# A fixed order of all tasks and loads in a fused retention and feed-forward kernel

## The chip, the cores and the metric

One core of a Trainium2 chip. The metric is the device time of one launch in microseconds (us): the median of three runs of the kernel before is 216.17 us, the runs lie between 215.56 and 217.98. The profiled run took 216.75 us and its span, from the first to the last instruction of the program, is 215.0 us.

## The reference

```
state = gamma * state + k[:, :, t] (outer) v[:, :, t]        # 4 batches, 8 heads, 768 steps, head size 64
y[:, :, t] = scale * q[:, :, t] @ state
x  = y as [4, 768, 512]                                       # heads side by side
xn = (x - mean(x)) / sqrt(var(x) + 1e-6) * g_ln
out = x + max(xn @ w_ch1, 0) @ w_ch2                          # w_ch1 512 x 2048, w_ch2 2048 x 512
```

Inputs and output are float32; the kernel works in bfloat16 with float32 sums.

## The kernel before, in words

**Tiles.** The 4 x 768 rows are cut into 24 tiles of 128 rows, t = 0 to 23: tiles 0 to 3 are the first chunk of each batch, tiles 4 to 8 are chunks 1 to 5 of batch 0, tiles 9 to 13 those of batch 1, and so on. The recurrence is worked in chunks: within a tile as a masked product, between tiles through a state.

**Tasks of one tile.** For t below 8 the tile's k and q are transposed on TensorE (PE) into PSUM (`tk` L440, `tq` L447) and copied out by ScalarE (`ek`) and VectorE (`eq` L452). From tile 8 on, k and q are loaded side by side into a buffer `qk` and transposed by a DMA issued by SyncE (`tr` L462). Then PE forms the scores (`pa` L480), VectorE masks them (`am` L491), PE forms the output y (`py`, L508 and, with a state, L504), VectorE takes mean and variance (`bn` L523, L524) and the shifted, scaled tile (`xn` L518), ScalarE keeps a copy of y (`xc` L529). The tile xn is transposed into a buffer `xnt`, on PE for t below 8 (`tx` L582, copy `ex` on ScalarE), by a SyncE DMA after that (`ex` L596). The state takes a product on GpSimd (`vg` L542), one on PE (`pd` L554) and one on VectorE (`pb` L568).

**The feed-forward.** Tiles are taken in 14 groups: eight of one tile, four of two, two of four. `m1(g, ho)` (L629) multiplies a group's xnt by a part of w1; each such task streams about 0.87 to 0.89 us of matmuls into one of two PSUM buffers `mm`. A `relu` task empties it into `h1` (ScalarE L642; for the first six groups ScalarE or VectorE L644). `m2(t)` (L667) multiplies h1 of one tile by w2 in four parts of four matmuls, into one of two PSUM buffers `tp`; VectorE adds the residual (`add` L676) and SyncE stores the tile (`st` L683). w1 and w2 come in four chunks each, W1_0 to W1_3 and W2_0 to W2_3; `m1(g, ho)` needs chunk W1_(ho/4), and the first part of any m2 needs all four chunks of w2.

**Loads.** GpSimd (POOL) issues all loads of k, q, v (L375, 128 KB each in bfloat16) and of w1 and w2 (L383, 512 KB each) into one queue. From tile 8 on, each load has a `gate` before it (L388): a tiny copy on POOL that waits until the load three earlier has landed. Only k and q of tile 0 come by the other queues, in two halves each, from SyncE and ScalarE (L346).

**Order.** The program has 818 tasks. Each is created by `a(...)` with the engine or engines that may run it, an estimated duration, a rank and its dependencies. `Plan.order` then places them one at a time: of all tasks that can start, it takes the one with the earliest estimated start, and among equals the lowest rank. The estimates add fixed margins for what a load or a DMA transpose may take (`load_pad`, `w_pad`, `tr_pad`, `x_pad`) and, for some tasks, a slack or a time before which they may not start (`slack`, `at`). The result is the order in which the instructions of each engine are written; on the chip an engine runs its own list in order and waits by semaphores. `Plan.fill` puts matmuls on zeros (`warm`, L694) into 80% of those gaps of PE that the plan shows in its first 14 us.

Of the kernel before, what the change touches and what calls it, by code (L numbers as in the profile page):

```python
# [14 lines left out]
PE, ACT, DVE, POOL, SP = range(5)  # L15
# [4 lines left out]
              "k3", "q3", "v3", "w1_2", "k4", "q4", "v4", "k5", "q5", "v5", "w1_3", "w2_0",  # L20
              "k6", "q6", "v6", "k7", "q7", "v7", "w2_1", "w2_2", "w2_3"],
    "bufs": {"qsb": 6, "ksb": 5, "vsb": 9, "qk": 8, "tr": 6, "vg": 3, "trq": 3, "trk": 3},
    "load_pad": 600, "w_pad": 1500, "lead": 32, "lead2": 32, "sq_at": 28000, "late_load": 1250, "tail": (0, 384, 512), "step": 8, "pace": 8, "ahead": 3,
    "slack": 600, "tr_pad": 4000, "x_pad": 3000, "vg_pad": 1000, "fill": 0.8, "fill_end": 14000,
}


class Plan:
# [20 lines left out]
        self.tasks.append(t)  # L49
        return t  # L50

    def order(self):
        left, ends = {}, {}
        for t in self.tasks:
            for u in t["uses"]:
                left[u] = left.get(u, 0) + 1
        held = {name: [] for name in self.bufs}
        engines = sorted(self.seen)
        free = dict(self.begin)
        todo = {e: [t for t in self.tasks if e in t["on"]] for e in engines}  # L60
        sw_free, hw_free, out = self.first_load, 0, []
        while any(todo.values()):
            best = None
            for e in engines:
                for t in todo[e]:
                    if any("end" not in d for d in t["after"] + t["follows"]):
                        continue
                    at = max(free[e], t["at"], sw_free - 7000 if t["load"] else 0)
                    for d in t["after"]:
                        if d["eng"] == e and not d["load"] and not d["hw"]:  # L70
                            at = max(at, d["end"])
                        else:
                            at = max(at, d["seen"] + t["slack"])
                    if t["takes"]:
                        name = t["takes"][0]
                        if len(held[name]) == self.bufs[name]:
                            oldest = held[name][0]
                            if left[oldest]:
                                continue
                            at = max(at, ends[oldest])  # L80
                    if best is None or (at, t["rank"]) < best[0]:
                        best = (at, t["rank"]), t, e
            if best is None:
                raise RuntimeError("no task can start")
            (at, _), t, e = best
            for x in t["on"]:
                todo[x].remove(t)
            t["eng"], t["start"], t["ns"] = e, at, t["on"][e]
            t["end"] = free[e] = at + t["ns"]
            t["seen"] = t["end"] + self.seen[e] + t["lat"]  # L90
            if t["load"]:
                sw_free = max(t["end"] + 800, sw_free) + t["load"]
                t["seen"] = sw_free + 700 + t["lat"]
            if t["hw"]:
                begun = max(at + 600, hw_free)
                queued = max(0, sw_free - begun)
                hw_free = begun + t["hw"] + min(queued, 2 * t["hw"])
                if queued:
                    sw_free += t["hw"] * 2 // 3
                t["end"] = free[e] = max(t["end"], hw_free - 900)  # L100
                t["seen"] = hw_free + 1050 + t["lat"]
            if t["takes"]:
                name = t["takes"][0]
                if len(held[name]) == self.bufs[name]:
                    held[name].pop(0)
                held[name].append(t["takes"])
            for u in t["uses"]:
                left[u] -= 1
                ends[u] = max(ends.get(u, 0), t["seen"])
            out.append(t)  # L110
        return out
# [16 lines left out]
def kernel(  # L128
# [28 lines left out]
    number = {bc: t for t, bc in enumerate(TILES)}  # L157
# [6 lines left out]
    FILL, FILL_END = CFG["fill"], CFG["fill_end"]  # L164
# [11 lines left out]
    plan = Plan({PE: 330, ACT: 130, DVE: 130, POOL: 130, SP: 0},  # L176
                {PE: 900, ACT: 800, DVE: 900, POOL: 840, SP: 740}, 3900)
# [18 lines left out]
    held = {}  # L196
# [93 lines left out]
    a = plan.add  # L290
# [105 lines left out]
    seq = [(x, t) for t in range(8) for x in "kqv"] + [("w1", j) for j in range(4)]  # L396
# [31 lines left out]
    for t in range(NT):  # L428
# [5 lines left out]
        slack = SLACK if t >= T0 else 0  # L434
# [25 lines left out]
        else:  # L460
            def e_tr(eng, t=t):
# [4 lines left out]
                   hw=1600, lat=TR_PAD)  # L466

            def e_eq(eng, t=t):
# [3 lines left out]
                   follows=[ams[-1]])  # L472
# [25 lines left out]
        def e_py(eng, t=t, c=c):  # L498
# [8 lines left out]
            for h in range(H):  # L507
# [7 lines left out]
                slack=slack)  # L515
# [76 lines left out]
        else:  # L592
            def e_ex(eng, t=t, xb=xb, xi=xi):
                if xi == 0:
# [4 lines left out]
                      follows=[ex[t - 1]] if xi else [])  # L599
# [95 lines left out]
                                 rhs=zeros[:, 0:w], start=True, stop=True)  # L695

    with tc.manual_schedule():
        for t in plan.fill(plan.order(), PE, 1100, FILL_END, FILL, warm):
            t["emit"](t["eng"])


# [28 lines left out]
```

## Time and profile before

| what | value |
|---|---|
| time, median of 3 | 216.17 us |
| span of the profiled run | 215.0 us |
| PE busy with matmuls | 206.0 us, 96% of the span, 1944 records |
| of it matmuls on zeros (L694) | 25 records, 7.3 us busy |
| VectorE, ScalarE, POOL busy | 118.2, 83.7, 97.7 us |
| POOL's load queue | 13.37 MB, 86.7% of 16 DMA engines' span |
| last load landed | about 141 us |

The profile counts a PE instruction as busy from its start to a modelled end, and neighbours overlap. The times at which successive matmuls start say more: the difference of two starts is what the first one really took from the end time. The second thing to look at is the idle time in brackets in the timeline, with what ended it.

### The profile page before, as it was taken

What the parts mean: (1) busy time and instruction counts of PE and PEld (TensorE: products, weight loads), DVE (VectorE), ACT (ScalarE), POOL (GpSimd) and SP (SyncE); (2) the same over time, 40 slices, a digit from 0 to 9 for tenths busy, and PEclk for the clock granted to TensorE, in tenths of its full rate; (3) what the DMA queues carried; (4) which work ended last, traced back from release to release, by engine and by line L of the source; (5) the groups of instructions that cost most, each with busy time, mean ns of one, the idle gap of its engine ahead of it and who ended that gap; (6) DMA issues with size and microseconds to landing.
All of it is one profiled execution on the core that took longest, in us unless ns stands there. A gap on an engine that the chain in (4) does not pass through costs nothing.

```text
span 215.0 us, 4757 instructions
## 1 busy us (share of the span) xinstructions
PE 206.0 (96%) x1944; PEld 132.5 (62%) x1964; DVE 118.2 (55%) x230; ACT 83.7 (39%) x157; POOL 97.7 (45%) x151
## 2 busy tenths in 40 slices
PE   7978999999999999999999999989999999999994
PEld 3457999998745558668567767645454544444443
DVE  6776688991178955186896857784164411011121
ACT  5366676665401106325325424305434214442000
POOL 8997779734767765686846485600000000000000
PEclk9999999999999999999999999999999999999999
DMA  8999999999899999999999999971112120010212
GB/s 125 174 180 180 164 195 169 208 118 138 90 155 179 179 173 203 145 166 136 149 139 179 139 172 164 148 181 26 24 49 73 27 98 19 30 47 5 98 49 98
DMA packets 108887, 26.82 MB, mean 125 GB/s; under 512 B 101569, under 2 KB 105921, under 8 KB 108866
## 3 DMA queue, kind: packets, MB, share of 16 engines
q0 software_dynamic: 77024, 13.37, 86.7%
q1 hardware_dynamic: 30642, 12.82, 27.8%
q10 hardware_dynamic: 1200, 0.33, 0.6%
q8 instruction: 15, 0.25, 0.4%
q14 instruction: 6, 0.05, 0.1%
HBM read 27.30 MB, written 6.29 MB: 156 GB/s over the span
## 4 chain that ended last, share of the span: by engine, by line
PE 82%; DMA 10%; POOL 5%; issue 1%; DVE 0%; POOLq 0%
PE tp L667 38%; PE mm L629 34%; DMA v<-in_v_dram 5%; DMA w<-in_moe_w_ch_dram 4%; PE pa L480 3%; PE pd L554 2%; PE py L508 2%; PE py L504 2%; POOL qsb L375 1%; DMA xnt<-xn 1%; POOL w L383 1%; POOL v L375 1%; POOL k L375 1%; POOL vg L542 0%; PE tp L582 0%
## 5 line engine op out<-in xcount | busy, mean ns | idle before, releaser
L629 PE MATMUL mm<-xnt,w 128*128 128x128 bf16 (+2 forms) x896 | 93.9, 257 | 1.4 <-ACT xnt L203 0.7
L667 PE MATMUL tp<-w,h 128*128 128x512 bf16 (+2 forms) x381 | 87.2, 370 | 1.3 <-issue 0.5
L642 ACT ACTIVATE h<-mm 128x512 bf16<-128x512 f32 x91 | 54.5, 598 | 72.9 <-PE mm L629 72.6
L629 PEld LDWEIGHTS <-w 128*128 128x128 bf16 x896 | 66.2, 98 | 21.5 <-issue 1.5
L667 PEld LDWEIGHTS <-h 128*128 128x128 bf16 x400 | 37.0, 98 | 38.3
L676 DVE SCALAR_TENSOR_TENSOR osb<-tp,rstd,x_all 128x512 f32<-128x512 f32 (+2 forms) x25 | 18.2, 729 | 48.1 <-PE tp L667 47.9
L491 DVE TENSOR_TENSOR asb<-pa,mask 128x1024 bf16<-128x1024 f32 x24 | 29.3, 1221 | 16.1 <-PE pa L480 16.1
L523 DVE BATCH_NORM_STATS2 bns<-py 128x6 f32<-128x512 f32 x24 | 16.7, 694 | 18.8 <-PE py L508 18.8
L529 ACT CAST x_all<-py 128x512 bf16<-128x512 f32 x24 | 14.0, 583 | 18.3 <-DVE xn L518 17.7
L542 POOL TENSOR_TENSOR vg<-vsb,vsc 128x512 bf16<-128x512 bf16 x16 | 16.6, 1044 | 6.0 <-DMA vsb<-in_v_dram 3.2
L375 POOL DMA_DIRECT2D vsb<-in_v_dram x20 | 18.3, 916 | 1.4 <-issue 1.4
L518 DVE SCALAR_TENSOR_TENSOR xn<-py,mv,gb 128x512 bf16<-128x512 f32 x24 | 18.0, 750 | 0.9
L568 DVE TENSOR_TENSOR state<-pd,gch 64x256 bf16<-64x256 f32 x40 | 16.7, 418 | 2.7 <-PE pd L554 2.4
L375 POOL DMA_DIRECT2D qk<-in_q_dram x16 | 14.0, 877 | 3.5 <-issue 2.8
L375 POOL DMA_DIRECT2D qk<-in_k_dram x16 | 14.1, 879 | 2.0 <-issue 1.7
L388 POOL COPY scrap<-qk 1x1 bf16<-1x1 bf16 x30 | 5.8, 194 | 16.3 <-DMA qk<-in_k_dram 8.6
L469 DVE TENSOR_TENSOR trq<-tr,qsc 128x512 bf16<-128x512 bf16 x16 | 7.9, 495 | 3.6 <-DMA tr<-qk 3.5
L604 ACT ACTIVATE rstd<-mv,epsb 128x1 f32<-128x1 f32 (+2 forms) x14 | 3.8, 289 | 13.7 <-DVE mv L524 13.7
L694 PE MATMUL pd<-zeros 128*128 128x512 bf16 (+1 forms) x25 | 7.3, 434 | 1.2 <-DVE zeros L238 1.2
L508 PEld LDWEIGHTS <-asb 128*128 128x128 bf16 x192 | 7.9, 98 | 0.5 <-issue 0.4
L508 PE MATMUL py<-vsb,asb 128*128 128x64 bf16 x160 | 7.9, 193 | 0.0
L504 PE MATMUL py<-state,trq 128*128 128x128 bf16 x80 | 7.7, 219 | 0.0
(64 smaller groups left out, 120.9 us busy)
## 6 DMA issues: line engine op xcount, KB each, us to landing
out_dram<-osb SPq DMA_DIRECT2D x23, 256.0 KB, 2.1
w<-in_moe_w_ch_dram POOLq DMA_DIRECT2D x8, 512.0 KB, 9.4
vsb<-in_v_dram POOLq DMA_DIRECT2D x20, 128.0 KB, 5.5
qk<-in_k_dram POOLq DMA_DIRECT2D x16, 128.0 KB, 4.8
qk<-in_q_dram POOLq DMA_DIRECT2D x16, 128.0 KB, 5.4
qsb<-in_q_dram POOLq DMA_DIRECT2D x7, 128.0 KB, 8.9
v<-in_v_dram POOLq DMA_DIRECT2D x4, 128.0 KB, 7.1
ksb<-in_k_dram POOLq DMA_DIRECT2D x4, 128.0 KB, 9.3
```

What stands on the lines that cost most here:

```text
L375: nc.gpsimd.dma_start(out=tile_of(kind, j), in_=src)
L491: nc.vector.tensor_tensor(out=take("asb", t, [P, NPAIR, 2, P], BF16).rearrange("p i a t -> p a i t"), in0=held["pa", t], in1=mask.rearrang ...
L508: nc.tensor.matmul(py[:, h, :], lhsT=held["asb", t][:, h // 2, h % 2, :], rhs=tile_of("v", t)[:, h, :], start=(mi == 0), stop=(mi == n - 1))
L518: nc.vector.scalar_tensor_tensor(out=take("xn", t, [P, DM], BF16), in0=held["py", t].rearrange("p h d -> p (h d)"), scalar=mv[:, t, 0:1], ...
L523: nc.vector.bn_stats(out=bns[:, t, :], in_=held["py", t].rearrange("p h d -> p (h d)"))
L529: nc.scalar.copy(out=x_all[:, t, :].rearrange("p (h d) -> p h d", d=D), in_=held["py", t])
L542: e.tensor_tensor(out=take("vg", j, [P, H, D], BF16), in0=tile_of("v", j), in1=vsc[:, cc, :].unsqueeze(2).to_broadcast([P, H, D]), op=ALU. ...
L568: nc.vector.tensor_tensor(out=held["pb", n][o, :, o], in0=held["pd", b][o, :, o], in1=gch[o, cc, :].unsqueeze(2).to_broadcast([D, NPAIR, D ...
L629: nc.tensor.matmul(p[:, j, :], lhsT=w1[:, ko, (ho + j) * P:(ho + j + 1) * P], rhs=held["xnt", hb][:, h0:h0 + n, ko, :], start=(ko == 0), s ...
L642: nc.scalar.activation(out=dst, in_=src, func=AF.Relu)
L667: nc.tensor.matmul(held[key], lhsT=held["h1", hb][:, ho, i * P:(i + 1) * P], rhs=w2[:, ho, cols], start=(ho == 0), stop=(ho == HO - 1))
L676: nc.vector.scalar_tensor_tensor(out=take("osb", key, [P, w], FP32), in0=held[key], scalar=rstd[:, t:t + 1], in1=x_all[:, t, cols], op0=AL ...
```

## The change: a list of 818 numbers in place of the rule

`Plan.order` no longer chooses. It walks through a list `ORDER` of all 818 tasks and writes them in that sequence. A number is the task's place in the order of creation; 10000 is added where a task that may run on two engines takes the second (VectorE for a relu). The list was found offline by exchanging tasks against the estimates of the plan. The estimates remain only to say how large PE's gaps in the first 14 us are, for `fill`; the margins `w_pad`, `tr_pad` and `x_pad` are made smaller, and `at` and `slack` no longer count. No instruction of the work is added or removed: 289 tasks on PE, 155 on ScalarE, 168 on VectorE, 146 on POOL and 60 on SyncE, as before. Eight relu tasks of the first six groups change engine, four each way.

```
-    "load_pad": 600, "w_pad": 1500, ...
-    "slack": 600, "tr_pad": 4000, "x_pad": 3000, "vg_pad": 1000, "fill": 0.8, "fill_end": 14000,
+    "load_pad": 600, "w_pad": 550, ...
+    "slack": 600, "tr_pad": 3000, "x_pad": 2000, "vg_pad": 1000, "fill": 0.8, "fill_end": 14000,
...
+ORDER = [int(x) for x in """
+15 18 14 23 3 8 19 2 27 24 13 26 22 25 44 16 17 45 0 4 7 6 5 28 146 20 21 9 147 10 149 1
+29 148 30 162 46 150 12 151 11 163 165 153 152 31 176 154 164 155 166 177 156 179 32 167
...
+""".split()]
...
-    def order(self):
+    def order(self, seq):
...
-        while any(todo.values()):
-            best = None
-            for e in engines:
-                for t in todo[e]:
...
-                    if best is None or (at, t["rank"]) < best[0]:
-                        best = (at, t["rank"]), t, e
...
+        for number in seq:
+            t = self.tasks[number % 10000]
+            e = sorted(t["on"])[number // 10000 % 10]
+            at = max(free[e], sw_free - 7000 if t["load"] else 0)
...
-        for t in plan.fill(plan.order(), PE, 1100, FILL_END, FILL, warm):
+        for t in plan.fill(plan.order(ORDER), PE, 1100, FILL_END, FILL, warm):
```

With the numbers turned into tasks, the lists of the engines differ as follows. `zero` is the clearing of the two state buffers (L288); `touch` is a small read of w1 that nobody waits for.

POOL, up to the loads of tile 8:

```
before: iota pos v0 k1 q1 v1 W1_0 k2 q2 W1_1 v2 k3 q3 v3 W1_2 zero vg0 k4 q4 v4 k5 q5 v5 W1_3
        W2_0 k6 q6 v6 k7 q7 v7 W2_1 vg4 vg5 W2_2 W2_3 vg6 k8 vg7 vg1 q8 v8 ...
after:  k1 pos iota q2 q1 zero k2 v0 v1 W1_0 W1_1 v2 k3 q3 W1_2 v3 k4 v4 q4 vg0 v5 k5 q5 W1_3
        vg4 q6 vg5 k6 v7 k8 v6 q8 k7 q7 W2_1 v8 W2_0 gate W2_3 vg6 vg7 vg1 gate W2_2 ...
```

PE, up to tile 3's output:

```
before: tk0 tq0 pa0 gb tk1 tq1 py0 pa1 tx0 py1 tk2 m1(0,0) tq2 pd0 tx1 pa2 m1(1,0) m1(0,4) py2
        tk3 m1(1,4) tq3 tx2 pa3 m1(2,0) m1(2,4) py3 ...
after:  tk0 tq0 tk1 pa0 gb tq1 tk2 py0 pa1 tq2 tx0 py1 m1(0,0) pa2 tx1 m1(0,4) py2 tk3 m1(1,4)
        tq3 m1(1,0) tx2 pd0 pa3 m1(0,8) m1(2,0) py3 ...
```

ScalarE's first tasks go from (k half, q half, powers of gamma for v and q, cast of k, cast of q) to (q half, k half, cast of k, cast of q, powers). SyncE loses `touch` from its start (it goes to a later place), and the transpose `ex` of tile 19, which stood behind `tr` of tiles 21, 22 and 23, now stands before `tr` of tiles 22 and 23; `tr` of tile 21 and `ex` of tiles 17 to 19 now stand behind the store of tile 13. Later on PE, two m2 tasks of different tiles are mixed part by part with each other and with m1 tasks, where before the four parts of one tile mostly followed one another; the first m2 stands behind `tx7` in both. The last twelve PE tasks are the same.

## Prediction

> **What bounds the kernel now.** I read the page's slices first, then PE's timeline, then the chain that ended last, then POOL's and SyncE's timelines at the few places where PE waited.
>
> ```profile
> PE   7978999999999999999999999989999999999994
> PEclk9999999999999999999999999999999999999999
> ```
>
> PE looks full from the third slice on, at full clock. So only the start and single holes can be won. How much work stands behind the nines I take from two pieces of the chain view (start, duration, what):
>
> ```profile
> 33.17 0.89 PE mm L629 x16
> 152.89 1.73 PE tp L667 x8
> ```
>
> 16 matmuls of 128 columns take 0.89 us (55.6 ns each) and 8 of 512 columns 1.73 us (216 ns each). Pricing every matmul but the zeros like this (with 0.43 us for a `pa`, which costs about 0.1 us more than its columns) gives 198.0 us of PE work. The last matmul ends at 211.9. So 211.9 - 198.0 = 13.9 us are not work. Where they lie is seen in PE's timeline (start, duration, instruction, idle before):
>
> ```profile
> 8.65 0.87 PE L694 MATMUL pd<-zeros 128*128 128x512 bf16 x3
> 9.78 0.88 PE L694 MATMUL pd<-zeros 128*128 128x512 bf16 x4
> 11.02 0.92 PE L694 MATMUL pd<-zeros 128*128 128x512 bf16 x5
> 14.72 0.38 PE L554 MATMUL pd<-vg,k 128*128 128x128 bf16 x4 [0.81 <-POOL vg L542]
> 18.21 0.39 PE L508 MATMUL py<-v,asb 128*128 128x64 bf16 x8 [0.26 <-DMA v<-in_v_dram]
> 20.40 0.40 PE L582 MATMUL tp<-idn,xn 128*128 128x128 bf16 x4 [0.39 <-DVE xn L518]
> 21.50 1.95 PE L629 MATMUL mm<-xnt,w 128*128 128x128 bf16 x32 [0.38 <-ACT xnt L203]
> 23.29 0.40 PE L508 MATMUL py<-v,asb 128*128 128x64 bf16 x8
> 32.79 0.38 PE L554 MATMUL pd<-vg,ksb 128*128 128x128 bf16 x4 [0.38 <-POOL vg L542]
> 143.64 1.89 PE L629 MATMUL mm<-xnt,w 128*128 128x512 bf16 x8 [0.65 <-DMA xnt<-xn]
> ```
>
> Up to 14 us PE streams zeros between small tasks. Then it waits several times until 21.5. After `py3` at 23.29 it is without a hole, but for two: by start-to-start times 0.54 us at 32.8 and 0.83 us at 143.6. About 12 us of the 13.9 thus lie before 23.29, and most of those are the arrival of data. The chain view says the same of the start, in its two longest pieces:
>
> ```profile
> 8.36 9.81 DMA v<-in_v_dram
> 21.06 9.23 DMA w<-in_moe_w_ch_dram
> ```
>
> v2 landed at 18.17, W1_3 at 30.28, each over 9 us after its issue: the queue is full, and one load follows another. POOL's timeline shows why no more is in flight:
>
> ```profile
> 12.56 1.10 POOL L288 MEMSET state<- 128x512 bf16 x2
> 18.45 0.88 POOL L375 DMA_DIRECT2D ksb<-in_k_dram  x1 [1.20 <-DMA v<-in_v_dram]
> 22.94 0.74 POOL L383 DMA_DIRECT2D w<-in_moe_w_ch_dram  x1 [1.09 <-DMA w<-in_moe_w_ch_dram]
> ```
>
> k5 waits for v2, W2_0 for W1_2: in both cases the load eight places earlier. So a load goes out when the eighth before it has landed. The hole at 143.6 is explained by SyncE's queue:
>
> ```profile
> 131.74 9.20 SPq L462 DMA_TRANSPOSE tr<-qk  x3
> 141.04 1.21 SPq L596 DMA_TRANSPOSE xnt<-xn  x1
> ```
>
> `ex19` stood behind three `tr`, the last of which waited for its q; PE waited for `ex19`.
>
> **What the Trainium skill says.** "Perfetto Trace Analysis", section Identifying the Most-Contended Engine, says that PE's busy share is a poor measure of distance to the bound; the trace agrees: 96% busy, 198.0 of 215.0 us (92%) work. "TensorE: Matmul & The Clock Gate", section Wait — 56ns, not 53.3ns?, gives 55.6 and 215.7 ns between warm matmuls of 128 and 512 columns, as here (55.6 and 216). The same page, section Step-by-step: what each phase is for, says that matmuls stay in program order; that is what makes a fixed order risky: one late operand holds up all behind it. "DMA: Bandwidth & Descriptors", section Queues, rings and completion order, says that each DMA engine takes turns between the queues; in this trace v0 landed 5.0 us after its issue while k0 and q0 came over other queues, k8 on the quiet queue 3.7 us after its own.
>
> **The change part by part.** PE's work stays 198.0 us, and so do the last twelve PE tasks and the 3.1 us from the last matmul to the end of the span. The end therefore moves by what the holes move.
>
> *Loads up to W1_2.* By the landings of single issues in the trace, a q, k or v follows its predecessor after 0.85 us and a weight chunk after 2.55 (v1 8.97, W1_0 11.50, k2 12.35, q2 13.19, W1_1 15.75). Between W1_1 and k3 (18.46) there is 1.0 us more than that; one instruction fetch of 16 KB ran on one DMA engine at 16.1 for 0.95 us. The new list has the same eight loads up to W1_1, so it should land near 15.7, and then v2, k3, q3, W1_2: one load (v3) fewer than before. W1_2 landed at 22.66, so now 22.66 - 0.85 = 21.8. k1 goes out at about 0.84 in place of v0 at 1.38, and `touch` leaves the start: up to 0.6 us earlier. Against it, `zero` (1.10 us) now stands between q1 and k2: k2 is issued about 5.2 and lands no earlier than 3.5 to 3.7 us later, 8.8, which is where the fourth load landed before (8.97). I take W1_2 at 21.2; bounds 20.3 (start gained and the fetch falling after it) and 21.8.
>
> *The first chain.* ScalarE's half of k goes out second and should land where q's did (4.78), not 3.85. The cast of k (0.60), of q (0.40), the powers (0.24 and 0.70) and `ek0` (0.58) then run one after another on ScalarE: `ek0` near 7.4 where it ended at 5.8; the table load of 1.28 us must also fit, hidden before 4.8 or, at worst, on this chain. The mask (1.22 on VectorE) follows, so `am0` moves from 7.03 to about 8.6 and `py0` from 8.4 to 10.0, which is about when v0 now lands (one load after k2: 9.7). `m1(0,0)` comes at about 13.4 (W1_0 13.2) against 12.63. This loss of 0.8 us is covered: `py2` cannot run before v2 at 17.2 to 18.2, and all up to `pa3` (about 3.4 us) fits before W1_2 arrives at 21.2.
>
> *From W1_2 on.* PE then has `m1(0,8)`, `m1(2,0)` ready, 2 x 0.89: `py3` at 21.2 + 1.78 = 23.0 with the same work behind it as at 23.29 before. Gain 0.3 us (bounds: gain 1.2, loss 0.3).
>
> *The two holes.* `pd4` no longer waits long: `vg4` runs after W1_3 is issued and v4 has landed (about 24.4 to 25.5), and PE reaches `pd4` at 25.4 by its work. `ex19` no longer stands behind q23: it follows the store of tile 13, whose last matmul PE reaches at about 133; issued near 139, landing 2.3 to 4 us later, it is needed at 146.5. Both holes go: 0.54 + 0.83 = 1.37 us.
>
> *New waits.* The first m2 needs all of w2. Before, W2_3 landed at 45.6 and m2 began at 49.6. Now k8, q8, v8 stand ahead (2.55 us) and `tr8` comes before it too: W2_2 lands at 48.2 to 49.5; PE is there at 49.0. Cost 0 to 0.6 us, I take 0.1. In between, `vg4` and `vg5` block POOL until v4 and v5 land, but eight loads are in flight. From tile 9 on, loads run ahead of PE by 5 us and more as before. Mixing m2 parts costs no matmul. The relus that change engine lie beside PE work.
>
> *Sum.* 216.17 - 0.3 - 1.37 + 0.1 = 214.6 us.
>
> **The rivals.** *A, an earlier start:* the instruction fetch falls elsewhere and the start gains its 0.6, so W1_2 lands at 20.3 and `py3` runs at 22.1: 216.17 - 1.2 - 1.37 = 213.6; with fewer waits in the first chain down to 213.0. For it: all waits before 21.5 end with DMA or a short chain behind one. Against: the eight-load window and `zero`. *B, new waits, slower:* the margins for transposes and weights are cut, and the list leaves no room where the estimate saw none. In this trace `tr` took 2.7 to 8.5 us to land and `ex` 2.3 to 6.6; if a late one holds PE at 3 to 4 of the 32 places for 1 us each, and the w2 wait costs 0.6: 214.6 + 4.1 = 218.7, a mild form 217. Against: for `pa` of tiles 12 to 20 loads land 3 us and more ahead before, and PE has other work in the list between. *C, nothing:* the late first chain costs 0.9 and m2's wait 0.5, which eats the holes: 216.17 - 1.37 + 1.4 = 216.2.
>
> **How the numbers follow.** Forecast 0.42, A 0.26, B 0.20, C 0.12. The range leaves out a fifth: from 213.0 (A) to 217.4 (mild B). Faster by over 1% means below 214.0: A, and a third of the forecast's spread of about half a us, 0.26 + 0.12 = 0.38. Slower by over 1% means above 218.3: most of B, 0.15. The rest, 0.47, lies within 1%.
>
> **What would show it.** Right: W1_2 landed near 21.2, `py3` on PE at 23.0, no bracket at `pd4` or at L629 behind `xnt` near 146, zero matmuls no more than now. Wrong: brackets on PE behind `tr`, `xnt` or w between 30 and 150 (B); `py3` before 22.3 (A) or after 23.6 (C); a piece of DMA w in the chain just before the first m2.

## The result, and the profile after

| us, but for the ratio | before | after |
|---|---|---|
| time, median | 216.18 us | 224.14 us |
| ratio, 95% interval | | 1.0335 (1.0275 to 1.0396) |
| span of the profiled run | 215.0 us | 222.4 us |
| first transpose of tile 0 on PE | 4.59 | 6.75 |
| W1_2 landed | 22.66 | 23.90 |
| `py3` on PE | 23.29 | 25.75 |
| last chunk of w2 landed | 45.59 | 57.01 |
| first m2 on PE | 49.55 | 57.65 |
| last matmul ends | 211.92 | 219.39 |

The kernel became slower by 3.35%. Its runs scatter more than those of before (four at 222.9 to 224.2, two at 228.1 and 229.3, which the ratio leaves out); the profile is that of a run of 224.2 us.

First the slices of the page, those of PE, of its clock and of the DMA engines:

```profile
PE   3798899994999999998999999999999999999994
PEclk9999999998899999999999999999999999999999
DMA  9999999999399999999999999699940112002032
GB/s 131 121 190 179 165 133 140 156 168 176 28 133 163 137 206 168 114 121 170 126 218 135 106 85 182 96 214 96 144 94 31 42 24 94 0 3 94 0 141 94
```

A slice is 5.56 us. PE is thin in the first slice and in the tenth (50 to 56 us); in the tenth and the one behind it its clock is below full. From 55.6 to 61.2 the DMA engines, full everywhere else up to 139 us, are three tenths busy and move 28 GB/s. Before had no such slice up to 139 us.

PE's timeline (start, duration, instruction, idle before and its end) gives the places:

```profile
6.75 0.61 PE L468 MATMUL tp<-idn,k 128*128 128x128 bf16 x4 [3.35 <-ACT k L231]
23.95 1.96 PE L657 MATMUL mm<-xnt,w 128*128 128x128 bf16 x32 [0.90 <-DMA w<-in_moe_w_ch_dram]
25.75 0.40 PE L536 MATMUL py<-v,asb 128*128 128x64 bf16 x8
28.21 0.39 PE L582 MATMUL pd<-vg,ksb 128*128 128x128 bf16 x4
...
53.45 0.40 PE L508 MATMUL pa<-trq,tr 64*128 64x128 bf16 x8 [3.13 <-DVE trq L497]
53.78 0.40 PE L582 MATMUL pd<-vg,k 128*128 128x128 bf16 x4
54.02 3.56 PE L657 MATMUL mm<-xnt,w 128*128 128x128 bf16 x32
57.37 0.45 PE L610 MATMUL tp<-idn,xn 128*128 128x128 bf16 x4
57.65 2.75 PE L695 MATMUL tp<-w,h 128*128 128x512 bf16 x12
...
102.00 1.03 PE L657 MATMUL mm<-xnt,w 128*128 128x256 bf16 x8 [0.58 <-DMA xnt<-xn]
```

`pd4` (28.21) has no bracket any more, and there is none near 146: the two holes of before are gone. New are 3.35 us before the first transpose, 0.90 for W1_2, 3.13 before `pa8`, and 0.58 at 102. After the wait at `pa8`, 32 matmuls of 128 columns took from 54.02 to 57.37, 105 ns each, where 32 at full clock took 1.79 us at 21.50 of before. The chain view has the transfers that PE waited for (start, duration, what):

```profile
12.07 11.84 DMA w<-in_moe_w_ch_dram
...
38.44 14.51 DMA tr<-qk
...
94.25 7.61 DMA xnt<-xn
```

The bracket at `pa8` names VectorE's `trq`, but that one began at 52.97, after 4.74 us of waiting for `tr8`. `tr8` took 14.51 us from issue to landing; its first packet moved 4.2 us after the issue, at 42.64. In the kernel before it took 4.80, and the longest of all `tr` 8.5.

So 2.46 us are lost up to `py3`, 5.64 more up to the first m2, and 0.63 are won from there to the last matmul (161.74 against 162.37). 2.46 + 5.64 - 0.63 = 7.47 us, the whole difference of the last matmuls. The 5.64 are the wait of 3.13, the half clock behind it (3.35 in place of 1.79: 1.56), `pa8` itself, which now stands ahead of the first m2 (0.33), and 0.6 us of small holes.

That arithmetic is true of this run. The experiments showed that it isn't the whole explanation: taking these pieces away one by one didn't bring the time back.

### The profile page after: what moved, and what is told of

Its sections match the earlier page's. It is cut to its first block, busy times and chain, and to the rows that moved or that the text cites. A ratio compares the mean times of both kernels' runs of the same rounds, so it can differ in the third digit from the quotient of the medians.

```text
span 222.4 us, 4762 instructions
## 1 busy us (share of the span) xinstructions
PE 208.9 (94%) x1970; PEld 135.0 (61%) x1970; DVE 118.6 (53%) x230; ACT 82.2 (37%) x157; POOL 97.3 (44%) x151
## 4 chain that ended last, share of the span: by engine, by line
PE 70%; DMA 18%; POOL 8%; issue 2%; DVE 1%; POOLq 0%
PE tp L695 36%; PE mm L657 27%; DMA tr<-qk 7%; DMA w<-in_moe_w_ch_dram 5%; DMA xnt<-xn 3%; DMA qk<-in_q_dram 2%; PE pa L508 2%; PE py L536 2%; POOL qsb L403 2%; PE pd L582 2%; PE py L532 2%; POOL k L403 1%; POOL v L403 1%; POOL w L411 1%; POOL vg L570 1%
## 5 line engine op out<-in xcount | busy, mean ns | idle before, releaser
L657 PE MATMUL mm<-xnt,w 128*128 128x128 bf16 (+2 forms) x896 | 97.6, 260 | 1.8 <-DMA w<-in_moe_w_ch_dram 0.9
L695 PE MATMUL tp<-w,h 128*128 128x512 bf16 (+2 forms) x400 | 92.1, 371 | 0.0
L657 PEld LDWEIGHTS <-w 128*128 128x128 bf16 x896 | 67.6, 99 | 24.2 <-issue 1.5
L416 POOL COPY scrap<-vsb 1x1 bf16<-1x1 bf16 x15 | 2.8, 189 | 22.9 <-DMA vsb<-in_v_dram 22.9
L638 DVE RECIPROCAL rstd<-rstd 128x1 f32<-128x1 f32 (+2 forms) x14 | 2.0, 154 | 18.8 <-ACT rstd L632 18.7
L722 PE MATMUL pd<-zeros 128*128 128x512 bf16 (+1 forms) x32 | 8.2, 401 | 1.2 <-DVE zeros L266 1.2
L508 PE MATMUL pa<-trq,tr 64*128 64x128 bf16 x128 | 6.4, 219 | 3.1 <-DVE trq L497 3.1
L508 PEld LDWEIGHTS <-tr 64*128 64x128 bf16 x128 | 3.7, 94 | 7.2 <-issue 4.0
## 6 DMA issues: line engine op xcount, KB each, us to landing
w<-in_moe_w_ch_dram POOLq DMA_DIRECT2D x8, 512.0 KB, 10.4
```

What stands on the lines that cost most here:

```text
L508: nc.tensor.matmul(pa[:, par, i, :], lhsT=held["trk", t][o, i, :] if t < T0 else held["tr", t][o, NPAIR + i, :], rhs=held["trq", t][o, i, ...
L657: nc.tensor.matmul(p[:, j, :], lhsT=w1[:, ko, (ho + j) * P:(ho + j + 1) * P], rhs=held["xnt", hb][:, h0:h0 + n, ko, :], start=(ko == 0), s ...
L695: nc.tensor.matmul(held[key], lhsT=held["h1", hb][:, ho, i * P:(i + 1) * P], rhs=w2[:, ho, cols], start=(ho == 0), stop=(ho == HO - 1))
```

## The experiments

Tasks are named as above. `move(tasks, before=x)` takes tasks out of the list and puts them ahead of task x; where lists of one engine are given, the others stay as they are. Times of before on the chips of the runs were 216.1 to 217.7 us; ratios are against them. A profile is that of one run, so the time is read from all runs of a kernel, and from the profile only where that one run waited.

### The table load: powers first (e1_powers_first)

ScalarE's timeline of after (start, duration, instruction):

```profile
4.78 1.28 ACT L231 ACT_TABLE_LOAD   x1 [4.78 <-DMA osb<-in_k_dram]
6.08 0.62 ACT L231 CAST k<-osb 128x512 bf16<-128x512 f32 x1
```

The load of the activation table, 1.28 us, stands directly ahead of the first instruction that computes, and behind that instruction's wait: here the cast of k, whose data landed at 4.71. In before the first computing instruction was the power for v, and the load ran while k was still under way:

```profile
1.88 1.28 ACT L267 ACT_TABLE_LOAD   x1 [1.88 <-issue]
```

"ScalarE: Activation LUTs", section What ACT_TABLE_LOAD costs, gives 1283 ns for this load, as here. The edit (9 is the power for v, 17 the cast of k; of the constants on VectorE the power needs 0 and 5, and 4, 7, 6 stand between them):

```diff
+move([0, 4, 7, 6, 5, 9], before=17)
```

> The changed order with ScalarE's first exponential (vsc) before the cast of k, so that the table load no longer stands between k's landing and the first transpose. First transpose near 4.9 us instead of 6.75 in both theories. Theory S (the start is bound by the load queue: W1_2 lands at 23.9): tile 3's py stays at 25.4 to 25.8, time 223.7 to 224.2 against 224.1. Rival (the first chain is the bound of the start): py of tile 3 near 23.9, time about 222.2.

Measured: 228.26 us (228.02 to 229.77), ratio 1.0548 (1.0498 to 1.0598). Both theories missed it. The start did become earlier: first transpose at 5.42 in place of 6.75, `py3` at 24.68, first m2 at 53.74 in place of 57.65. (The rest of the way to the 4.59 of before is ScalarE's half of k, which goes out second: it landed at 4.67, in before at 3.85.) And the time rose by 4 us. PE's timeline of this kernel shows where, then SyncE's queue:

```profile
97.55 1.03 PE L705 MATMUL tp<-w,h 128*128 128x512 bf16 x4
103.89 1.86 PE L667 MATMUL mm<-xnt,w 128*128 128x256 bf16 x8 [5.32 <-DMA xnt<-xn]
105.55 1.91 PE L705 MATMUL tp<-w,h 128*128 128x512 bf16 x4
```

```profile
92.89 1.24 SPq L500 DMA_TRANSPOSE tr<-qk  x1
94.17 0.57 SPq L721 DMA_DIRECT2D out_dram<-osb  x1
94.79 2.64 SPq L634 DMA_TRANSPOSE xnt<-xn  x2
```

The 0.58 us at 102 of after has become 5.32, and the slices show the clock at half around it: four m2 matmuls take 1.7 us in place of 0.86. The queue gives the reason. The two `xnt` are `ex10` and `ex11`; they stand behind `tr14` (92.89), and `tr14` waited for its q, which landed at 92.74. Then the two share the DMA engines with two loads and a store: the second landed 7.6 us after its issue, at 103.8. In after PE came to this place 2.9 us later (101.4 against 98.6) and the second `xnt` landed 1.9 us earlier (101.9), and so the wait was small. Two limits stood one behind the other, and the first hid most of the second. Why the q of tile 14 landed later here (92.74 against 90.83 in after), though the start was earlier, isn't shown.

### w2 ahead of tile 8 (e2_w2_before_tile8, e2b_chain8_late)

```diff
+move([40, 41, 42, 49, 48, 51, 50], before=52)   # v6 k7 q7 and all of w2 ahead of k8
+move([55], before=57)                           # gate k8
+move([276], before=684)                         # eq8, pa8, am8, py8 ... behind the first m2
+move([277], before=674)
+move([278], before=685)
+move([279, 280, 281], before=296)
```

> The changed order with all of w2 loaded before k, q, v of tile 8, as in the kernel before, and with eq, pa, am, py of tile 8 placed after the first m2 parts. Theory W (the transpose of tile 8 beside the w2 loads holds up both itself and w2): W2_2 lands near 48.7 instead of 57.0, the 3.1 us wait in front of pa goes, the first m2 starts near 52.4 instead of 57.65; time about 219.3. Rival (the loads lag for another cause, POOL standing at its copies and gates): w2 still lands after 54 and the time stays over 221.5.

Measured: 227.99 us (227.31 to 228.41). `tr8`, now behind the last chunk of w2, took 2.81 us in place of 14.51; W2_2 landed at 50.37 in place of 57.01; no wait at `pa8`. Of the 6.6 us that W2_2 gained, 2.55 are the three loads that now stand behind it; the rest, about 4, is an estimate of what `tr8` cost. And again the time rose, to the rival's side: the wait for `xnt` is 5.09 us here, at 104.8. In this profile PE also reached full clock only near 19 us, so that `py3` came at 28.50 and the first m2 at 54.71, not at 52.4. The second half of the edit alone, `pa8` and its followers behind the first m2 with the loads as in after:

> The changed order with only eq, pa, am, py of tile 8 placed after the first m2 parts; the loads stay as changed. Theory W: the wait in front of pa is replaced by a wait of the first m2 for w2, which lands near 57: m2 starts near 57.2, PE idles some 4.7 us before it and runs cold after it; time 223 to 224.1. Rival (the place of pa is the whole cause): m2 starts near 52.4, time about 219.3.

Measured: three runs at 228.31 to 230.55 us and one at 223.32. The runs of after are spread alike (222.9 to 229.3), so this half alone isn't shown to cost or to gain time. The profile, of the run of 228.31, has 4.98 us at the same place, and it shows one thing more:

```profile
51.26 2.75 PE L708 MATMUL tp<-w,h 128*128 128x512 bf16 x11
56.34 2.75 PE L708 MATMUL tp<-w,h 128*128 128x512 bf16 x12 [2.33 <-DMA w<-in_moe_w_ch_dram]
```

W2_0 landed at 51.22 and m2 started; it then waited for W2_2, which landed at 56.30. On the chip a part of an m2 waits for its own chunk only. That the first part of any m2 needs all four chunks, as the words on the kernel before have it, holds for the plan's estimate, not for the semaphores.

### The touch of w (e3_touch_first)

```diff
+move([145], before=3)     # touch back to SyncE's start
```

> The changed order with the small read of w1 back at its early place on SyncE. In the changed kernel W1_0 landed 3.63 us after v1, in the kernel before 2.53. Theory T (the early read of w1 makes the first chunk quick): W1_0 lands 2.6 us after v1, all loads behind it about 1.1 us earlier, W1_2 near 22.8, time about 223.1. Rival (the 1.1 us have another cause): W1_0 still 3.6 us after v1, time 224.1 or slightly more for the DMA time of the small read.

Measured: three runs at 226.04 to 230.31 us and one at 222.64, again spread like those of after, so no change of the time is shown. In the profile W1_2 landed at 22.88, as the theory had it, but not for its reason: W1_0 came 3.35 us after v1. In four kernels below that have the first loads of before and `touch` at its early place (e5, e11, f2, f3) it came 3.0 to 4.3 us after v1; an early `touch` doesn't make the chunk quick.

The profile, of the run of 226.04, has 4.35 us behind `xnt`. Of the five profiles so far, the four with a wait of 4.4 to 5.3 us belong to runs of 226.0 to 228.4 us, the one with 0.58 to a run of 224.2. It may be that the slower runs of after have this wait too; no two profiles of one kernel show it.

### Half of the change alone (e5_new_compute_only, e6_new_loads_only)

If the two queues that issue transfers were at fault, their old order under the new order of PE, ScalarE and VectorE should mend it, and the other half should break it.

```diff
-GpSimd and SyncE: lists of after
+GpSimd and SyncE: lists of before
```

> The list of after for PE, ScalarE and VectorE; GpSimd (loads, gates, value gates) and SyncE (transposing transfers, stores) in the order of before. Theory Q (the loss sits in the orders of the two queues that issue transfers): W2_3 lands near 46 again, no wait for xnt over 1 us between 90 and 110; what stays is the late start (py3 near 24.5) and up to 2 us at pa8, whose tr8 the old queue issues at 47: 217 to 219.5. Rival K (PE meets its operands too early because of its own new order): 222 or more.

> The order of before on every engine but GpSimd, which has that of after. Theory Q: W1_2 lands near 23.9, w2 is complete only near 55 to 57, so the first m2 comes 6 to 7 us later than the 49.55 of before, and the later loads are 5 us and more behind: 221 to 225. Rival K (the order of loads does no harm, PE's order does): 216 to 218.

Measured: 233.46 us (ratio 1.0756, 1.0674 to 1.0839) and 241.17 us (1.1096, 1.1023 to 1.1168). Both halves are worse than the whole, so the first theory fell. In the first kernel, GpSimd's old list has a `vg` in front of loads that must wait for a `pd` of PE's new list: 32.5 us in eight waits. In the second, PE's two longest waits are these:

```profile
85.31 0.58 PE L580 MATMUL pd<-vg,qk 128*128 128x128 bf16 x4 [6.36 <-POOL vg L568]
...
165.31 3.21 PE L655 MATMUL mm<-xnt,w 128*128 128x512 bf16 x8 [7.23 <-DMA xnt<-xn]
```

The old PE list wants a `vg` that GpSimd's new list has behind a gate, and an `ex` that stands in SyncE's queue behind three `tr` (issued from 146.84 to 162.61) whose loads come late (the last load landed at 161 us against 141 in before). The new lists fit one another and not the old ones. A half of such a change says little of what that half is worth.

### The queue: `ex10` and `ex11` ahead of `tr14` (e7_x_before_tr14)

With the powers first, as in the first experiment:

```diff
 SyncE: ... st3
-       tr14 st4 ex10 ex11 st5 ...
+       st4 ex10 ex11 tr14 st5 ...
```

> The kernel with the powers first (228.26), and in SyncE's queue ex10 and ex11 ahead of tr14. Theory X (ex10 and ex11 stood behind tr14, which waited for q14, and then shared the DMA engines with two loads; that wait of 5.3 us and the cold clock after it, 1.7 us, took back what the earlier start had won): no wait for xnt between 95 and 105, 220.5 to 222. Rival L (the loads themselves run 7 us late, so the next tile's operands hold PE in place of these): 224 to 228.

Measured: 223.54 us (221.83 to 226.76), ratio 1.0261 (1.0164 to 1.0358) against 1.0548 with the powers alone; two of the four runs lie in the theory's 220.5 to 222. The wait for `xnt` is gone. SyncE's queue:

```profile
87.53 3.06 SPq L622 DMA_TRANSPOSE xnt<-xn  x2
91.94 1.23 SPq L488 DMA_TRANSPOSE tr<-qk  x1
```

`ex10` and `ex11` go out 7 us earlier. `tr14`, behind them, costs nobody anything: in after it landed at 94.9 for a `pa14` at 108.

### w2 first, the queue mended (e8_w2_first_and_x)

The queue's edit, the powers first, `pa8` and its followers behind the first m2, and on GpSimd:

```diff
-  ... q6 vg5 k6 v7 k8 v6 q8 k7 q7 W2_1 v8 W2_0 gate(k8) W2_3 vg6 vg7 vg1 gate(q8) W2_2 gate(v8) k9 v9 q9 ...
+  ... q6 vg5 k6 v7 v6 k7 q7 W2_1 W2_0 W2_3 W2_2 k8 q8 v8 vg6 vg7 vg1 gate(k8) k9 gate(q8) q9 gate(v8) v9 ...
```

> As the run before it, and the four w2 chunks ahead of the three loads of tile 8, pa8 and what follows it after the first m2, and each gate of tile 8 directly ahead of the load that it paces. Theory X plus the w2 theory: w2 complete near 50, first m2 near 51.5, loads of tile 9 near 56, 218 to 219.5. Rival L: 221 or more, with waits for tr or xnt after 90.

Measured: 222.55 us, ratio 1.028 (1.0194 to 1.0367), which the last kernel's interval covers; rival L was right. The first m2 comes at 51.0 in place of 56.06, but of these 5 us 1 is left in the median and nothing in the two profiles (the last matmul ends at 217.3 and 217.1). They went into waits of 1.48 us at 81 and 1.30 at 115, both for `xnt`, and some smaller ones. The loads had fallen behind again: load 46 of the queue (counted from 0) landed at 86.49 (before: 77.18), load 63 at 123.02 (before: 112.67), though those of tile 9 had started only 3 to 4 us later than before.

### The gates (e9_even_gates, e12_powers_and_gates)

Why loads fall behind can be read from the list. A gate, which stands before every load from tile 9 on, waits for the load of the same kind of the tile before. In before, gate and load alternate, and three loads are in flight. In after the gates are mixed:

```
before:  gate(k11) k12  gate(q11) q12  gate(v11) v12  gate(k12) k13 ...
after:   gate(k11) k12  gate(v11) gate(q11) v12  gate(k12) q12  k13  gate(v12) gate(q12) q13  v13 ...
```

Ahead of q12 stands the gate that waits for k12, just issued: at that moment only one other load can be under way. For each of the 48 loads from k8 on, those that the gates allow in flight at once can be counted in the list (a load that a gate has seen landed counts as landed with all before it): three for 46 of them in before; in after three for 26, two for 19, one for 3. The edit, made in the kernel of the last experiment, puts each gate directly ahead of the load it paces and leaves the order of the loads; three may then be in flight at 38 (27 without it):

```diff
-gate(k11) k12  gate(v11) gate(q11) v12  gate(k12) q12  k13 ...
+gate(k11) k12  gate(v11) v12  gate(q11) q12  gate(k12) k13 ...
```

> As e8_w2_first_and_x, but each gate of GpSimd stands directly ahead of the load that it paces, through the whole list, as in before; the loads keep the order of after. Theory P (the new list mixes gates and loads so that often only one or two paced loads are in flight where before had three, and the stream of loads falls back by 10 us until 120): load 46 lands near 79 instead of 86.5, load 63 near 115 instead of 123, no wait for xnt over 1 us, 219 to 220. Rival R (the DMA engines are busy anyway and set the pace): landings within 2 us of those of e8, 222 to 223.

Measured: 218.81 us (217.27 to 219.63), ratio 1.0117 (1.0064 to 1.017); 3.7 us less than with mixed gates, and the two intervals don't meet. GpSimd's timeline with mixed gates, and with even gates, at the same place:

```profile
71.17 0.18 POOL L414 COPY scrap<-qk 1x1 bf16<-1x1 bf16 x1 [3.19 <-DMA qk<-in_q_dram]
...
80.64 0.18 POOL L414 COPY scrap<-qk 1x1 bf16<-1x1 bf16 x1 [4.23 <-DMA qk<-in_q_dram]
81.11 0.87 POOL L401 DMA_DIRECT2D qk<-in_q_dram  x1 [0.29 <-issue]
```

```profile
75.77 0.18 POOL L414 COPY scrap<-qk 1x1 bf16<-1x1 bf16 x1 [2.61 <-DMA qk<-in_q_dram]
76.24 0.87 POOL L401 DMA_DIRECT2D qk<-in_q_dram  x1 [0.29 <-issue]
```

Load 46 is issued at 76.24 in place of 81.11 and lands at 81.97 (79 was expected), load 63 lands at 116.90 in place of 123.02. From the first m2 on PE's timeline has no bracket over 0.3 us: 161.6 us to the last matmul, against 162.37 in before.

The same edit of the gates on the kernel with the powers first, where w2 is late and `ex10`, `ex11` stand behind `tr14`:

> As e1_powers_first (228.26), and only the gates moved, each directly ahead of the load that it paces; w2 stays late and ex10, ex11 stay behind tr14. Theory P (thin loads are the root: q14 comes late, tr14 waits for it, ex10 and ex11 wait behind tr14): q14 lands 4 us earlier than the 92.7 of e1, the wait for xnt of 5.3 us is gone or below 1 us, first m2 still near 54, 220 to 221.5. Rival X (the place in SyncE's queue is a cause of its own): the wait stays at 2 us and more, 223 or more.

Measured: 223.4 us (222.04 to 225.85). q14 landed 1.9 us earlier than in the first experiment, not 4, and the wait for `xnt` fell from 5.32 to 1.97 us. Neither theory alone was right: in these profiles even gates remove most of the wait, and moving `ex10`, `ex11` removes all of it.

### The start (e10_zero_late, f1_start_loads, f2_powers_late, f3_tr8_beside_w2)

The kernel with even gates, the clearing of the state (`zero`) behind the first loads, nearly as in before, and `touch` back ahead of `tr8`:

```diff
 GpSimd:
-  k1 pos iota q2 q1 zero k2 v0 v1 W1_0 W1_1 ...
+  k1 pos iota q2 q1 k2 v0 v1 W1_0 W1_1 ... v3 zero k4 ...
```

> As e9_even_gates, with the memset of the state after the loads of the start instead of between q1 and k2, and the touch of w ahead of tr8. Theory Z (the memset and the short loads ahead of it leave the load queue thin from 6 to 11 us, which makes W1_2 late): W1_2 lands 1 us earlier than in e9 and py3 runs 0.7 to 1 us earlier; the time falls by as much. Rival: py3 stays, since the chain of the first tiles or the cold clock sets it; no change within 0.5 us.

Measured: 217.34 us (216.25 to 219.78), ratio 1.0059 (1.0029 to 1.0089). Its interval and that of the kernel without this edit (1.0064 to 1.017) touch, and the profile doesn't show what was expected: v1 lands 1.1 us earlier (10.59), but W1_0 at 15.64 (14.83 without the edit), W1_2 at 23.41 (22.70), `py3` at 25.25 (24.55). So whether this edit gains is not settled, and not by the way that was expected.

Then single early steps of the change in an otherwise unchanged kernel before:

```diff
 f1  GpSimd, up to W1_3:
-    iota pos v0 k1 q1 v1 W1_0 k2 q2 W1_1 v2 k3 q3 v3 W1_2 zero vg0 k4 ...
+    k1 pos iota q2 q1 zero k2 v0 v1 W1_0 W1_1 v2 k3 q3 W1_2 v3 k4 v4 q4 vg0 ...
 f2  ScalarE:
-    k half, q half, powers, cast of k, cast of q
+    q half, k half, cast of k, cast of q, powers
 f3  GpSimd:
-    v7 W2_1 vg4 vg5 W2_2 W2_3 vg6 k8 vg7 vg1 q8 v8
+    v7 k8 q8 W2_1 vg4 vg5 W2_2 W2_3 vg6 vg7 vg1 v8
```

> The order of before on all engines, but GpSimd's list up to the issue of W1_3 is that of after (k1 q2 q1, the clearing of the state, k2 v0 v1 W1_0 W1_1 v2 k3 q3 W1_2 v3 ...). Theory: this order alone makes W1_2 late (23.4 or later against 22.66), because the first short loads are issued too slowly to keep the queue full; py3 moves by 0.7 to 1.5 and the time to 217 to 218. Rival: W1_2 lands as in before or earlier, and the time stays within 0.5 us of before.

> The order of before, but ScalarE begins as in after: q half, k half, cast of k, cast of q, then the powers. Theory: the activation table is loaded only when the second half of k has landed (from 4.8 us instead of 1.9), the first transpose moves from 4.6 to 6.7, and py3 by 1 to 2 us: 217 to 218.5. Rival: the arrival of v2 and W1_2 covers it (py3 within 0.4 us), the time stays within 0.5 us of before.

> The order of before, but k8 and q8 are loaded ahead of W2_1, so that tr8 is issued near 40 and runs beside the last three chunks of w2. Theory: tr8 takes 10 us or more in place of 4.8, W2_3 lands at 50 to 53 in place of 45.6 and holds the first m2 (49.55 before): 218 to 221. Rival: both transfers take their usual time, W2_3 lands 1.7 us later (two loads of 0.85), before PE needs it: 216 to 217.

Measured:

| | time, ratio (95%) | what the trace shows |
|---|---|---|
| f1 | 222.16, 1.0253 (1.0206 to 1.03) | W1_0 at 15.22 (before 11.50), W1_2 at 23.49 (22.66); `py3` at 30.45 |
| f2 | 218.58, 1.0095 (1.0058 to 1.0131) | first transpose at 6.62, `py3` at 26.17 |
| f3 | 221.52, 1.0228 (1.0173 to 1.0283) | `tr8` 10.44 us; W2_3 at 49.17 (45.59); first m2 at 53.98 |

f2 is the clear one: ScalarE's new start costs 2 us by itself (1.3 to 2.8 by the interval), and the arrival of v2 and W1_2 doesn't cover it (W1_2 landed at 23.15). The table load stands at 4.66, behind the wait for k, as in after. The edit holds two delays: by the first transposes of after, the first experiment and before (6.75, 5.42, 4.59) the table load is 1.3 us of the way, the later half of k 0.8.

f1 confirms that this order of loads makes the w1 chunks late, but its 5.5 us aren't the price of that: PE's old list met `vg0`, which the new order has three loads later, with a wait of 3.52 us, and from 18.9 to 25.7 it ran at half clock. f3 shows `tr8` slow again beside w2; its time, however, comes mostly from another place, 3.06 us at `pd4`, since `vg4` now stands behind a W2_1 that is issued later. Neither time is a measure of the step.

### The two holes (e11_before_two_holes)

The one part of the change for which the prediction had a gain, put alone into before:

```diff
 GpSimd:
-  ... v7 W2_1 vg4 vg5 ...
+  ... v7 vg4 W2_1 vg5 ...
 SyncE:
-  ... ex18 tr21 tr22 tr23 ex19 st11 ...
+  ... ex18 tr21 ex19 tr22 tr23 st11 ...
```

> The order of before in every place but two: vg4 ahead of the issue of W2_1 on GpSimd, ex19 ahead of tr22 in SyncE's queue. The prediction's step: both holes (0.54 at pd4, 0.83 at the m1 behind ex19) go, 1.37 us less than the kernel before on this chip (0.9 to 1.5). Rival: the next operand is no earlier, so the holes only move; within 0.4 us of before.

Measured: 215.29 us (20 runs, 214.77 to 216.59) against 216.12 (37 runs): ratio 0.9967 (0.9949 to 0.9985). Both holes are gone in the profile, and from the first m2 to the last matmul PE takes 161.4 us in place of 162.37. This is the only kernel here that is faster than before, by 0.8 us; the 0.9 to 1.5 of the prediction's step were missed. Its `py3` came at 24.23, 0.9 later than in the profile of before, with the same first loads: W1_0 landed 4.31 us after v1, in before 2.53.

## Why the prediction was wrong

**PE's work, right.** From the first m2 on, after needs no more time than before (161.74 and 162.37 us, with a wait of 0.58 in the former), and with the waits mended 161.4 to 161.6.

**The two holes, right in kind.** Both are gone in after; alone they are worth 0.8 us (0.3 to 1.1 by the interval) where the prediction put 1.37.

**Loads up to W1_2, wrong.** 21.2 was predicted with an upper bound of 21.8; measured 23.90. The list of after lands W1_2 at 22.7 to 23.9 in the twelve profiles that have its start, the list of before at 21.9 to 23.2 in five: the new start is no gain but a loss, and single runs differ by 1.3 us either way. What failed is the rule that a load follows its predecessor after 0.85 or 2.55 us, read from one profile. Three steps of after took more: v0 1.97, W1_0 3.63, W1_2 3.68. The first is `zero`: the prediction asked only when k2 lands (8.8 forecast, 8.66 measured), not what the gap does to the loads behind. From 6 to 11 us before moved 154, 161, 187, 201 and 186 GB/s, after 122, 117, 81, 120 and 145. But `zero` isn't the whole cause. With `zero` out of the gap (e10) the queue moved 144 to 157 GB/s there, v1 came 1.1 us earlier than without that edit, and W1_0 only 5.05 us after it. W1_0 also took 3.0 to 4.3 us in the four other profiles with the first loads of before. At W1_2 an instruction fetch of 16 KB fell, at 20.7; the prediction had named that fetch, and its lower bound let it fall behind W1_2.

**The first chain, wrong in its size.** The prediction left open whether the table load is hidden or on this chain. It was on it: `m1(0,0)` came at 16.49 in place of 13.4. In after the loss was still covered, by the late W1_2, for which PE waited 0.90 us; with the loads of before it isn't, and f2 has it at 2 us. PE also reached full clock at 9.7 us in place of 6.2, and 32 matmuls on zeros ran in place of 25, against the sign "no more than now"; what these two cost isn't shown.

**The first m2, wrong, and this is the step that was farthest off.** "W2_2 lands at 48.2 to 49.5" took `tr8` as free for the loads, and gave `tr8` no price of its own. W2_2 landed at 57.01, `tr8` at 52.95. The transfer and the queue slowed each other. DMA queues of before from 37 to 44, where the last chunks of w2 are loaded alone, and of after from 43 to 50, beside `tr8` (packets, MB, share of 16 engines):

```profile
q0 software_dynamic: 1668, 1.41, 126.7%
```

```profile
q0 software_dynamic: 1096, 0.91, 89.5%
q1 hardware_dynamic: 887, 0.23, 36.8%
```

In the same 7 us the load queue moved 0.91 MB in place of 1.41. "DMA: Bandwidth & Descriptors", section Queues, rings and completion order, says that each engine takes turns between queues at the grain of a packet. The counts of the profile agree with turns one for one: 1096 packets of 830 bytes on average for 887 of 260, and from 45 to 50, when `tr8` was under way all the time, 732 for 726. The prediction had cited this very sentence and drew from it only what v0 lost at the start. (The load that it calls k8 there, 3.7 us on a quiet queue, is k9.) From landings, v8 lost 4.4 us: it came 5.21 us after its predecessor, where a full queue took 0.85. W2_1 lost 1.4 (3.93 in place of 2.55), but ahead of `tr8`'s first packet, and 2.4 in the kernel that has no `tr8` there (e2); that part has another cause, which is open. The experiments hold the step up: `tr8` took 10 us or more in all eight kernels that issue it beside the w2 loads, f3 among them, whose list is otherwise that of before, and 2.8 to 6.1 in the nine that issue it behind them. The estimate in the kernel's own code, which the list was fitted to, has `tr8` landed at 40.9 with its margin and W2_2 at 47.4.

That the first m2 needs all of w2 failed too: `m2(2)`'s first part, which comes first in after, needs W2_0 alone (51.92). The late w2 itself held PE nowhere in after; what held it was `tr8`. The loads of tile 9 stood in line behind w2 and came 5 us late.

**"From tile 9 on, loads run ahead of PE by 5 us and more as before", wrong.** That was a sentence without working. The new list of gates lets fewer loads be in flight, so these 5 us were never made up: the last load of a tile landed 3.5 to 5.0 us later than before for tiles 9 to 14, 7.6 to 10.0 for tiles 15 to 21, and the last of all at 161.6 in place of 140.7. With even gates, in the kernel that has the other edits too, it is 2.4 to 4.9 and 3.7 to 6.5. The late loads made `ex10` and `ex11`, behind `tr14` in SyncE's queue, the next limit.

**The rivals.** B was the right kind: brackets on PE behind `tr` and `xnt` appeared between 30 and 150, as its test said; the one behind w came at 23.95. `py3` after 23.6, which came too, was the sign of C. B's size, 218.7, came from three or four waits of 1 us out of 32; there were few waits, but long ones, and most waits over 3 us were followed by a half clock. Its argument against, "loads land 3 us and more ahead before", was taken from a trace of the old list. A and C were wrong.

**What stays open.** The kernel with all of this mended (217.34) is still above before by 0.3 to 0.9%; its loss lies before the first m2, which comes at 51.47 in place of 49.55. How much of that is the list isn't settled by single profiles, since `py3` moves by 0.9 us with the same first loads (e11). Why W1_0 takes 2.5 to 5.1 us after v1, with the old loads and with the new, isn't explained by these runs, nor why W2_1 takes 3.9 and 5.0 after q7. What each edit is worth in the last kernel wasn't tested by taking it out.

## What to carry to other kernels

A list of orders is only as good as the estimate behind it. Here the estimate put too low what a transposing transfer and the loads cost each other, and it counted the table load as a task of its own at the start, where it stands behind the wait of the first activation. And the list moved gates past one load, which leaves fewer loads in flight; a free exchange of tasks uses up exactly the margins that guard against such things. When an experiment takes away the first wait and the time doesn't fall, look for the next wait in the trace before giving up the theory: the powers first, and w2 first, each made the kernel slower alone, and both are part of the kernel that is 6.8 us faster than after. And read an in-order queue from the back: for each transfer ask what the one ahead of it waits for, and who needs it sooner.

## What the runs showed of the hardware

- `tr8`, a transposing transfer of 128 x 1024 numbers (256 KB), took 13.1 to 14.9 us beside the w2 loads in seven kernels, 10.4 in an eighth, and 2.8 to 6.1 behind them in nine. In the eight, 3.9 to 4.5 us passed between its issue and its first packet, in the nine 1.3 to 2.3. Small packets in one queue and large ones in another were not shared by bytes: 0.70 MB against 0.19 in the same 5 us.
- After the wait of 3.13 us at `pa8` and after waits of 4 to 5 us near 100, matmuls ran at half clock for 3 to 7 us. "TensorE: Matmul & The Clock Gate", section Part 1: The HAM clock gate (the "warmup" mystery), says that the clock falls after an idle window of about 3.4 us that runs freely. Here shorter waits were enough: 3.13 us in after, where the half clock added 1.6 us to the wait, and 2.18 at `pa8` of e7. Waits of 2.19, 2.33 and 2.35 us in three other kernels (e12, e2b, e1) were not followed by it, so the length alone doesn't decide.
- With the same first tasks PE reached full clock at 9.7 us in after and near 19 us in the kernel with w2 ahead of tile 8: `py3` at 25.75 and at 28.50.
